# A decode-attention block rebuilt: 32 KB runs for the cache loads, value matmuls on four column groups, and an MLP tail with stationary weights

## The chip, the cores and the metric

The kernel runs on one core of a Trainium2 chip. The metric is device time in microseconds (us); a number for a kernel is the median of its runs. The profile's span is about 1.9 us shorter than that time, because it runs from the first to the last instruction.

## The reference

A batch of 8 single tokens passes an adaptive LayerNorm, attention over a cache of 8,192 positions (32 query heads, 8 key/value heads), an output projection, a second adaptive LayerNorm and an MLP with a squared ReLU.

```python
mod = (silu(c) @ w_mod)                       # six vectors of 512 per token
h = layernorm(x) * (1 + ca) + sa
q = h @ wq                                    # 8 x 32 heads x 128
k, v = repeat(k_cache, 4), repeat(v_cache, 4) # each cache [8, 8, 8192, 128] bf16
o = softmax(q k^T / sqrt(128)) v
x = x + ga * (o @ wo)                         # 4096 -> 512
h = layernorm(x) * (1 + cb) + sb
out = x + gb * (relu(h @ w1 + b1)**2 @ w2 + b2)   # 512 -> 1792 -> 512
```

Each cache holds 134 MB, so the kernel has to move about 284 MB, nearly all of it keys and values that are used once.

## The kernel before

One load is one head of one batch row: 2 MB, in which each of the 128 partitions takes one contiguous run of 16 KB. There are eight ring slots.

```python
src_ap = A_k_cache[kind[1], kind[2]].rearrange("(p t) d -> p t d", p=128)   # values likewise
dst_ap = RING[s][:, :, :]
# ...
ins = sp.dma_start(dst_ap, src_ap)
```

Keys are transposed on TensorE (PE), copied out of PSUM by VectorE (DVE) and ScalarE (ACT), and multiplied with the queries. For the values, each of the 64 tiles of a head is one matmul whose stationary side has four columns (the four query heads that share the values) and whose moving side is 128 columns of V.

```python
for t in range(NT):                                    # 64 tiles per head
    # ... a wait
    qt = (t // 4) % 4
    ins = pe.matmul(Ob[32 * gq:32 * gq + REP, co:co + 128],
                    Pm[:, t, 32 * qt + REP * g:32 * qt + REP * (g + 1)],
                    RING[s][:, t, :], start=(t == 0), stop=(t == NT - 1), tile_position=(0, 32 * gq))
```

The tail keeps the 8 tokens on 8 partitions. The activations are stationary, the weights move, and "fillers" (matmuls whose result nobody reads) keep PE busy between the small steps.

```python
dve.tensor_tensor(t1[:], attn_ps, mod_sb[:, 2 * D:3 * D], ALU.mult)        # 8 x 512
# ... residual and LayerNorm: eight more DVE steps, one ACT step, all on 8 partitions
pe_fill(pe, 48)
# ... four transposes, copy to hbT
for ci, (f0, fl) in enumerate(f_chunks):
    for kt in range(KT_D):
        ins = pe.matmul(hid_flat[:, f0:f0 + fl], hbT[:, kt, :], W1v[:, kt, f0:f0 + fl], ...)
# ... ReLU on ACT, square on DVE, 14 transposes, copy to hidT
for kt in range(KT_F):
    ins = pe.matmul(mlp_ps, hidT[:, kt, :], W2v[:, kt, :], start=False, stop=(kt == KT_F - 1))
```

## Time and profile before

| | before |
|---|---|
| time, median | 703.65 us (703.32 to 704.1, four runs) |
| span of the profiled run | 701.7 us |
| steady rate, 60 to 609.5 us | 426 GB/s |
| instruction packets of the PE queue | 80 |
| last packet of the last value load | 674.1 us |
| from there to the end | 27.6 us |

The landing in the table comes from the trace's packet records (the end of the last packet of that load, counted from the start of the span). It is the number to watch: until it, the kernel waits for data, after it, for the chain of small steps.

These lines are from the page of the kernel before: busy time of the engines, the rows of DMA busy share and rate in 40 slices of the span, and the DMA queues (packets, megabytes, share of the 16 engines' span).

```profile
PE 617.2 (88%) x10113; PEld 528.0 (75%) x10113; DVE 324.6 (46%) x594; ACT 177.7 (25%) x217; POOL 6.2 (1%) x25
DMA  9999999999999999999999999999999999999950
GB/s 354 430 372 429 423 427 425 424 425 428 428 423 425 427 427 424 427 425 426 425 425 426 425 427 423 428 427 424 427 425 425 423 430 424 426 426 427 412 208 1
q1 hardware_dynamic: 26020, 283.68, 96.2%
q8 instruction: 80, 1.31, 0.8%
```

PE is busy 88% of the time, but the DMA engines are busy over 90% in each of the first 38 slices, and from the second slice on the rate stands near 426 GB/s. The third slice (372) holds the load of the output projection's weights, in runs of 1 KB.

The next view cuts the same trace into stretches. Its columns are the stretch, its length, busy time of PE, PEld, DVE, ACT and POOL, the granted PE clock, the DMA share and GB/s.

```profile
60.00:609.50 549.50, 502.13 (x8402) 437.74 (x8400) 260.69 (x466) 146.20 (x180) 0.00 (x0) 0.97 1.01 426
670.00:676.00 6.00, 6.00 (x114) 5.74 (x111) 0.82 (x4) 0.00 (x0) 0.00 (x0) 1.00 0.52 212
676.00:682.00 6.00, 6.00 (x107) 5.61 (x105) 0.72 (x3) 0.00 (x0) 0.00 (x0) 1.00 0.54 191
```

From 670 to 682 us the DMA share is about one half.

How PE handles the values is in one line of the groups (line, engine, operation, output<-inputs, shapes, count; busy time and the mean of one; idle time before):

```profile
L579 PE MATMUL PS<-ring,KTb 128*4 128x128 bf16 x4096 | 221.6, 219 | 8.8 <-DVE rinv L563 5.3
```

There are 4,096 of them with four stationary columns each. Some lines of the timeline of the kernel before show its tail (columns: start, duration, engine, line, operation, output<-inputs, count; in brackets the idle time before it and what ended that).

```profile
682.80 1.89 PE L634 MATMUL PS<-wo_sb,oTn 128*8 128x512 bf16 x8
...
685.89 0.68 DVE L705 BATCH_NORM_STATS2 stats<-x 8x6 f32<-8x512 bf16 x1
...
689.38 3.19 PE L755 MATMUL PS<-ring,hbT 128*8 128x512 bf16 x16
```

The second layer (line 796) is another 14 matmuls of 512 columns in 3.19 us.

### The profile page before, as it was taken

The page shows a single profiled execution, that of the slowest core. Times are in us where ns is not written, and L with a number is a line of the kernel's source. Part 1 is how long each engine was busy: PE and PEld are TensorE (multiplying, and loading weights), DVE is VectorE, ACT ScalarE, POOL GpSimd, SP SyncE. Part 2 cuts the span into 40 slices and gives each one's busy share as a digit, 9 for nine tenths or more (in the row PEclk, how much of TensorE's full clock was granted, in tenths as well). Part 3 has the DMA queues.
Part 4 walks back from the last instruction along what each step waited for, and adds up shares of the span by engine and source line. Part 5 has one row for each costly group of instructions (what it writes and reads, how often), then busy time and mean ns, then how long its engine had stood idle before and what let it go on. Part 6 is the DMA issues. An engine that isn't in the chain of part 4 may idle for free.

```text
span 701.7 us, 21480 instructions
## 1 busy us (share of the span) xinstructions
PE 617.2 (88%) x10113; PEld 528.0 (75%) x10113; DVE 324.6 (46%) x594; ACT 177.7 (25%) x217; POOL 6.2 (1%) x25
## 2 busy tenths in 40 slices
PE   0499799997989799997999899897989989997998
PEld 0187699776977699776987699776977689775984
DVE  1357612774057621766046720676027820676213
ACT  1024510443024410433013320344014420244101
POOL 3000000000000000000000000000000000000000
PEclk9979999999999899999999989999999999999999
DMA  9999999999999999999999999999999999999950
GB/s 354 430 372 429 423 427 425 424 425 428 428 423 425 427 427 424 427 425 426 425 425 426 425 427 423 428 427 424 427 425 425 423 430 424 426 426 427 412 208 1
DMA packets 26109, 285.05 MB, mean 406 GB/s; under 512 B 2187, under 2 KB 8100, under 8 KB 9125
## 3 DMA queue, kind: packets, MB, share of 16 engines
q1 hardware_dynamic: 26020, 283.68, 96.2%
q8 instruction: 80, 1.31, 0.8%
q14 instruction: 9, 0.07, 0.0%
HBM read 283.66 MB, written 0.01 MB: 404 GB/s over the span
## 4 chain that ended last, share of the span: by engine, by line
PE 49%; DMA 38%; DVE 10%; ACT 2%; issue 1%; SPq 0%
DMA ring<-in_A_k_cache_dram 30%; PE PS L439 23%; PE PS L579 14%; PE PS L477 6%; DMA ring<-in_A_v_cache_dram 5%; DVE KTb L413 5%; DMA ring<-in_w_mod_dram 3%; DVE m L501 2%; ACT P_sb L528 2%; PE PS L551 2%; PE PS L292 1%; PE PS L634 1%; PE PS L333 1%; DVE mod_sb L300 0%; PE PS L796 0%
## 5 line engine op out<-in xcount | busy, mean ns | idle before, releaser
L413 DVE COPY KTb<-PS 128x1024 bf16<-128x1024 bf16 x432 | 270.9, 684 | 80.7 <-PE PS L439 79.8
L439 PEld LDWEIGHTS PS<-IDENT,ring 128*128 128x128 bf16 x4096 | 230.7, 98 | 63.1 <-DMA ring<-in_A_k_cache_dram 35.3
L439 PE MATMUL PS<-IDENT,ring 128*128 128x128 bf16 x4096 | 251.2, 220 | 12.9 <-DMA ring<-in_A_k_cache_dram 11.8
L420 ACT ACTIVATE KTb<-PS 128x1024 bf16<-128x1024 bf16 x144 | 147.5, 1024 | 445.2 <-PE PS L439 423.5
L579 PE MATMUL PS<-ring,KTb 128*4 128x128 bf16 x4096 | 221.6, 219 | 8.8 <-DVE rinv L563 5.3
L579 PEld LDWEIGHTS PS<-ring,KTb 128*4 128x4 bf16 x4096 | 218.3, 85 | 10.7 <-DVE rinv L563 6.2
L596 DVE CAST O_sb<-PS 128x256 bf16<-128x256 f32 x7 | 3.0, 425 | 196.3 <-PE PS L579 196.3
L477 PE MATMUL PS<-KTb,QTm 128*32 128x512 bf16 x1024 | 78.8, 384 | 5.3 <-ACT KTb L420 5.3
L551 PE MATMUL PS<-IDENT,P_sb 128*128 128x128 bf16 x512 | 45.1, 271 | 10.2 <-ACT P_sb L528 10.0
L551 PEld LDWEIGHTS PS<-IDENT,P_sb 128*128 128x128 bf16 x512 | 42.8, 126 | 11.8 <-ACT P_sb L528 10.7
L477 PEld LDWEIGHTS PS<-KTb,QTm 128*32 128x32 bf16 x1024 | 15.7, 94 | 21.5 <-DVE KTb L413 9.0
L528 ACT ACTIVATE P_sb<-PS,negm 128x512 bf16<-128x512 f32 x32 | 21.5, 685 | 22.9 <-DVE negm L519 22.9
L501 DVE TENSOR_REDUCE m<-PS 128x1 f32<-128x512 f32 x32 | 19.8, 680 | 0.0
L292 PE MATMUL PS<-ring,csT 128*8 128x512 bf16 x24 | 8.0, 511 | 10.6 <-DMA ring<-in_w_mod_dram 10.6
L609 DVE CAST O_sb<-PS 4x128 bf16<-4x128 f32 x8 | 2.3, 287 | 26.6 <-PE PS L579 26.6
L292 PEld LDWEIGHTS PS<-ring,csT 128*8 128x8 bf16 x24 | 2.5, 107 | 15.7 <-issue 14.6
L511 PEld LDWEIGHTS PS<-Dm,R 128*128 128x128 bf16 x8 | 0.8, 96 | 17.3 <-DVE Dm L505 17.3
L511 PE MATMUL PS<-Dm,R 128*128 128x4 bf16 x8 | 1.4, 179 | 13.3 <-DVE Dm L505 13.3
L535 DVE TENSOR_REDUCE rs<-rs 128x1 f32<-128x4 f32 x8 | 1.3, 157 | 22.8 <-ACT P_sb L528 22.8
L300 DVE CAST mod_sb<-PS 8x3072 bf16<-8x3072 f32 x1 | 3.3, 3345 | 17.5 <-PE PS L292 17.5
L276 PE MATMUL PS<-IDENT,cs 8*128 8x8 bf16 x4 | 0.3, 167 | 10.4 <-DVE cs L250 10.4
L715 ACT ACTIVATE std_<-std_ 8x1 f32<-8x1 f32 x1 | 0.2, 202 | 34.5 <-DVE std_ L709 34.5
(87 smaller groups left out, 98.9 us busy)
## 6 DMA issues: line engine op xcount, KB each, us to landing
ring<-in_A_k_cache_dram SPq DMA_DIRECT2D x64, 2048.0 KB, 30.7
ring<-in_A_v_cache_dram SPq DMA_DIRECT2D x64, 2048.0 KB, 35.0
ring<-in_A_wq_dram SPq DMA_DIRECT2D x2, 2048.0 KB, 9.7
wo_sb<-in_A_wo_dram SPq DMA_DIRECT2D x1, 4096.0 KB, 24.7
ring<-in_B_w_dram SPq DMA_DIRECT2D x2, 1792.0 KB, 24.9
ring<-in_w_mod_dram SPq DMA_DIRECT2D x2, 1536.0 KB, 16.5
x_sb<-in_A_x_dram SPq DMA_DIRECT2D x1, 8.0 KB
c_sb<-in_c_dram SPq DMA_DIRECT2D x1, 8.0 KB
```

The source lines that it names most:

```text
L292: ins = pe.matmul(mod_ps[:, j, :], csT[:, kt, :], wmod_view(kt, j), start=(kt == 0), stop=(kt == KT_D - 1))
L300: s_dve.inc(dve.tensor_copy(mod_sb[:], mod_ps.rearrange("b k n -> b (k n)")))
L333: ins = pe.matmul(QT_ps[:, h, :], wq_view(kt, h), haT[:, kt, :], start=(kt == 0), stop=(kt == KT_D - 1))
L413: v = s_edve.inc(dve.tensor_copy(dst, STG[seq % NSTG]))
L420: v = s_eact.inc(act.activation(dst, STG[seq % NSTG], ACT.Copy))
L439: ins = pe.matmul(STG[seq % NSTG][:, i, :], RING[s][:, t, :], IDENT[:, :], is_transpose=True)
L477: ins = pe.matmul(S_ps[32 * q:32 * (q + 1), k, :], QTm[:, b, g, :], KTb[:, 512 * cch:512 * (cch + 1)], start=(g == 0), stop=(g == HKV - 1) ...
L501: s_dve.inc(dve.tensor_reduce(m4[:, k:k + 1], S_ps[:, k, :], AX.X, ALU.max))
L528: ins = act.activation(P_sb[:, k, :], S_ps[:, k, :], ACT.Exp, bias=negm[:, 0:1], scale=inv_sqrt, accum_out=rs4[:, k:k + 1])
L551: ins = pe.matmul(STG[seq % NSTG][:, i, :], P_sb[:, k, j0:j0 + 128], IDENT[:, :], is_transpose=True)
L579: ins = pe.matmul(Ob[32 * gq:32 * gq + REP, co:co + 128], Pm[:, t, 32 * qt + REP * g:32 * qt + REP * (g + 1)], RING[s][:, t, :], start=(t ...
L634: ins = pe.matmul(attn_ps, oTn[:, h, :], wo_view(h), start=(h == 0), stop=(h == HQ - 1))
```

## The change

The intent is threefold. Two heads are loaded as one 4 MB unit whose runs are 32 KB per partition. Four tiles of values are multiplied by one matmul: 32 stationary columns (four tiles times eight query heads), 512 moving columns, and four such matmuls on the four column groups of the array; a small matmul with a selection matrix then picks the products that belong together. And the tail is transposed: features lie on 128 partitions, the weights are stationary and eight columns move. The program is also written through a helper that places the semaphore waits. The file is nearly all new; this is the core of the difference, with cuts.

```diff
-src_ap = A_k_cache[kind[1], kind[2]].rearrange("(p t) d -> p t d", p=128)
+src = (A_k_cache if kv == "k" else A_v_cache)[b, 2 * p:2 * p + 2]
+src = src.rearrange("g s d -> (g s d)").rearrange("(p f) -> p f", p=128)     # 32 KB a partition, four slots
 # ... value matmuls
-for t in range(NT):
-    ins = pe.matmul(Ob[32 * gq:32 * gq + REP, co:co + 128], Pm[:, t, ...], RING[s][:, t, :], ...)
+for m in range(32):
+    cg = m % 4
+    t = op("tensor", ... e.matmul(Obank[32 * cg:32 * (cg + 1), :], lhs[:, p, 32 * m:32 * m + 32],
+           vt[:, 4 * m:4 * m + 4, :], start=(m < 4), stop=(m >= 28), tile_position=(0, 32 * cg)), ...)
 # ... the very last unit: V stationary, eight columns moving, in chunks of 64, 32, 16, 16 tiles as they land
+pe_fill(70)
+for i, t1 in enumerate(CH):
+    for m in range(t0, t1):
+        t = op("tensor", ... e.matmul(oT_ps, vt[:, m, :], lhs[:, p, 8 * m:8 * m + 8], ...), ...)
+    if i == 0:
+        before_last()        # projection of units 0, 1, 2, and the biases
+    elif i == 1:
+        pe_fill(8)
 # ... MLP
-ins = pe.matmul(hid_flat[:, f0:f0 + fl], hbT[:, kt, :], W1v[:, kt, f0:f0 + fl], ...)
+t = op("tensor", ... e.matmul(hT_ps[hh][:, f % 7, :], wcol(k), hbT[:, k, :], ...), ...)
-ins = pe.matmul(mlp_ps, hidT[:, kt, :], W2v[:, kt, :], ...)
+for cc in range(2):
+    t = op("tensor", ... e.matmul(y_ps[64 * cc:64 * (cc + 1), :], hidT[:, f, :],
+           W2v[:, f // 2, f % 2, 256 * cc:256 * (cc + 1)], ..., tile_position=(0, 64 * cc)), ...)
```

## The prediction

> **What bounds it now.** The DMA. The stage view shows 425 to 426 GB/s in every 78.5 us stretch from 60 to 610 us (one batch row, 33.6 MB, each), with the DMA share at 1.01. The Trainium skill, "DMA: Bandwidth & Descriptors", section "Where 436 GB/s comes from", gives 435 GB/s as the ceiling; the trace agrees. PE is also busy 72 of each 78.5 us, but that is nearly hidden. Two things cost beyond streaming:
>
> 1. Eight of the 16 DMA engines finish late. DMA share is 1.04 at 660 us, about 0.5 from 670 to 682, then zero. The instruction queue moved 80 packets of 16 KB, about 1.07 us each, 86 us in all: if they sit on those eight engines that is 10.7 us each, about the lag. The lagging engines set every landing.
> 2. The tail. The last V load lands near 675.5 us on the slow engines; the kernel ends at 701.7. Those 26 us are PE value matmuls (3.75 us per head, catching up since the softmax at 651), projection, LayerNorm on 8 partitions (DVE 0.4 to 0.7 us per op), MLP with 8 rows stationary (3.2 us per layer), fillers, transposes, output DMA 1.8 us.
>
> **What the change does.**
>
> - Runs of 32 KB. Packet records: 16 KB takes 613 ns, 8 KB 309, 1 KB 49: an estimate from these is 602 ns per 16 KB plus 11 fixed. The skill page, section "Why small descriptors are slow", also names a fixed cost per packet. 512 fewer packets per engine x ~10 ns = about -5 us, all on the critical path.
> - Value matmuls: 128 of 58 ns per pair of heads (7.5 us) become 32 of 512 columns on four column groups, estimated 2 to 3.5 us from the score matmuls (8 in 0.61 us). PE falls from ~72 to ~55 us per batch row: off the critical path, except for the last batch row's backlog.
> - Instructions: my count is about 15.7k instead of 21.5k, so instruction packets shrink by a quarter: about -3 us on the slow engines.
> - Start: two small loads go ahead of the weights, +0.8 us. wo still has 1 KB runs (348 GB/s at 40 to 52 us): unchanged.
> - Tail: last V landing moves to about 668.5 us. From there PE does the rest of the filler, chunk 0, early projection (96 matmuls at 28 ns, as the Q projection's 128 in 3.58 us), last chunks, late projection (about 7 us together), then about twelve small ops on 128 partitions at 0.15 to 0.35 us (3 us), W1 1.6 us, squares 0.4, W2 about 1.2, two adds 0.6, output 1.9: about 16 us. Beside it w1 and w2 land about 9.4 us after V, and need 5 more: nearly as long. Tail saved: about 10 us.
>
> **Sum.** -5 -3 +1 -10 = about -17 us: 686.5 us (-2.4%), range 681 to 692.
>
> **Right if:** steady rate rises to about 429 GB/s; instruction queue near 60 packets; PE busy share falls to 55-65% with granted clock low in value phases; about 16 us between last V landing and end. **Wrong if:** 32 KB packets take twice 613 ns, or HBM dislikes the new pitch (rate below 425); PE in the key phase (10 us per 4 MB against 9.75 us of DMA) gets a cold clock from the idle value phases and falls behind, starving the four-slot ring; the filler of 70 matmuls delays the last unit; or the w2 landing is later than thought.
>
> Chances: faster by over 2%: 0.72; within 2%: 0.25; slower: 0.03.

## More of the kernel before

A load has sixteen landing marks in the trace, one for each DMA engine, and it has landed when the last has come. Of the marks of the last value load, eight came between 658.4 and 663.8 us and eight between 672.9 and 674.6: half of the engines are late by more than 10 us.

The projection ends at 684.7, 10.6 us after the last value landed, because PE still had value matmuls to catch up on. The MLP part takes the last 17.0 us.

## The result

| | before | after |
|---|---|---|
| time, median | 703.65 us | 690.88 us (689.68 to 691.25, four runs) |
| span of the profiled run | 701.7 us | 689.1 us |
| steady rate, 60 to 609.5 us | 426 GB/s | 430 GB/s |
| instruction packets of the PE queue | 80 | 58 |
| last packet of the last value load | 674.1 us | 665.6 us |
| from there to the end | 27.6 us | 23.5 us |

The ratio is 0.9816, with a 95% interval of 0.9802 to 0.983. A ratio here is the mean time of one kernel's fast runs over the mean of the other's fast runs of the same rounds, so it is not quite the ratio of the medians. The kernel is 1.8% faster. All outputs are right. It lies inside the predicted range, but 4.4 us above its centre, and just outside the class that had been favoured (faster by over 2%).

The two landings split the gain: 8.5 us come from data that arrive earlier, 4.1 us from a shorter tail (27.6 less 23.5).

The lines of the page of the kernel after that answer to those above:

```profile
PE 501.7 (73%) x7476; PEld 358.5 (52%) x7476; DVE 300.8 (44%) x557; ACT 235.1 (34%) x281; POOL 17.8 (3%) x67
GB/s 349 442 365 434 429 431 432 427 432 428 425 434 432 432 426 427 429 426 434 435 430 427 430 425 431 433 428 434 425 435 424 428 432 431 433 430 424 421 312 28
q1 hardware_dynamic: 15940, 283.67, 96.7%
q8 instruction: 58, 0.95, 0.6%
```

The same megabytes went in 15,940 packets instead of 26,020, and the rate is some 4 GB/s higher. The slice of the 1 KB runs is as slow as before (365). The stretches of the kernel after, with the columns as above:

```profile
60.00:609.50 549.50, 410.26 (x5837) 285.85 (x5837) 248.84 (x448) 195.89 (x234) 0.00 (x0) 0.82 1.00 430
670.00:676.00 6.00, 3.99 (x110) 3.66 (x107) 0.00 (x0) 0.00 (x0) 0.00 (x0) 0.59 0.36 136
676.00:682.00 6.00, 4.76 (x97) 4.29 (x95) 1.85 (x10) 0.90 (x3) 0.00 (x0) 0.50 0.01 3
```

The value matmuls are now a group of 992 (the last unit, in the thin form, is not among them), which took less than half of the time; the selection matmuls add 22.6 us:

```profile
L442 PE MATMUL PS<-ring,Pm 128*32 128x512 bf16 x992 | 88.3, 519 | 51.7 <-DMA ring<-in_A_v_cache_dram 47.4
```

In the steady part PE works 92 us less, and nothing is gained or lost by it: the DMA share is still 1.00. But the granted clock is down to 0.82, and in the tail, where before it was 1.00, it is 0.5 from 671 us on.

The timeline of the kernel after, from the arrival of the first chunk of the last values to the end:

```profile
661.46 5.37 PE L340 MATMUL PS<-IDENT 128*128 128x128 bf16 x70
666.67 1.75 PE L506 MATMUL PS<-Pm,ring 128*128 128x8 bf16 x64
668.28 2.33 PE L478 MATMUL PS<-oTn,wo_sb 128*128 128x8 bf16 x87
672.62 0.38 PE L478 MATMUL PS<-oTn,wo_sb 128*128 128x8 bf16 x9 [2.01 <-issue]
...
674.62 1.01 PE L340 MATMUL PS<-IDENT 128*128 128x128 bf16 x8
...
676.75 1.02 PE L478 MATMUL PS<-oTn,wo_sb 128*128 128x8 bf16 x32 [0.29 <-DVE oTn L514]
...
681.41 1.68 PE L558 MATMUL PS<-hbT,ring 128*128 128x8 bf16 x56
...
683.02 3.20 PE L566 MATMUL PS<-ring,hidT 128*64 128x256 bf16 x28
```

Three things stand out. The 70 fillers run from 661.5 to 666.8, although the first chunk of values had landed at about 661.2. In the middle of the projection PE stands still for 2.01 us, and the trace gives no instruction as the cause: "issue" means that PE waited for nothing that the profile shows. And the second MLP layer takes 3.20 us, as long as before, although two column groups share its columns.

The tail of 23.5 us is then: the rest of the fillers 1.1, the first chunk and the early projection 3.9, the standstill 2.0, the rest of the projection and the biases 1.1, the other three chunks with eight fillers 2.8, normalisation and late projection 1.3 (together 12.2); the small steps 3.1; a wait behind 16 more fillers 0.4; the first MLP layer 1.7; the second 3.2; the two last DVE steps 0.95; the output 1.9.

### The profile page after: what moved, and what is told of

The parts are those of the page before. It is cut to its first block, busy times and chain, and to the rows that moved or that the text cites. A ratio compares the mean times of both kernels' runs of the same rounds, so it can differ in the third digit from the quotient of the medians.

```text
span 689.1 us, 16075 instructions
## 1 busy us (share of the span) xinstructions
PE 501.7 (73%) x7476; PEld 358.5 (52%) x7476; DVE 300.8 (44%) x557; ACT 235.1 (34%) x281; POOL 17.8 (3%) x67
## 3 DMA queue, kind: packets, MB, share of 16 engines
q1 hardware_dynamic: 15940, 283.67, 96.7%
## 4 chain that ended last, share of the span: by engine, by line
PE 54%; DMA 39%; DVE 3%; ACT 2%; issue 1%; SPq 0%
PE PS L348 35%; DMA ring<-in_A_k_cache_dram 34%; PE PS L363 9%; DMA ring<-in_A_v_cache_dram 4%; PE PS L442 4%; PE PS L405 3%; PE PS L340 1%; ACT KTb L353 1%; ACT P_sb L396 1%; DVE Pm L418 1%; DVE m L368 1%; PE PS L423 1%; PE PS L478 1%; PE PS L506 0%; PE PS L566 0%
## 5 line engine op out<-in xcount | busy, mean ns | idle before, releaser
L353 ACT ACTIVATE KTb<-PS 128x1024 bf16<-128x1024 bf16 x192 | 196.5, 1024 | 384.2 <-PE PS L348 384.2
L348 PE MATMUL PS<-IDENT,ring 128*128 128x128 bf16 x4096 | 267.5, 227 | 49.2 <-DMA ring<-in_A_k_cache_dram 49.2
L355 DVE COPY KTb<-PS 128x1024 bf16<-128x1024 bf16 x320 | 210.1, 688 | 149.5 <-PE PS L348 147.2
L442 PE MATMUL PS<-ring,Pm 128*32 128x512 bf16 x992 | 88.3, 519 | 51.7 <-DMA ring<-in_A_v_cache_dram 47.4
L451 DVE CAST O_sb<-PS 128x512 bf16<-128x512 f32 x31 | 21.4, 692 | 132.5 <-PE PS L442 132.5
L442 PEld LDWEIGHTS PS<-ring,Pm 128*32 128x32 bf16 x992 | 30.8, 121 | 90.2 <-DMA ring<-in_A_v_cache_dram 48.5
L454 PE MATMUL PS<-SEL,O_sb 128*128 128x8 bf16 x124 | 22.6, 182 | 30.4 <-DVE O_sb L451 24.8
L454 PEld LDWEIGHTS PS<-SEL,O_sb 128*128 128x128 bf16 x124 | 12.2, 98 | 59.5 <-DVE O_sb L451 46.1
L405 PE MATMUL PS<-IDENT,P_sb 128*64 128x128 bf16 x512 | 25.7, 276 | 10.3 <-ACT P_sb L396 10.0
L405 PEld LDWEIGHTS PS<-IDENT,P_sb 128*64 128x64 bf16 x512 | 22.1, 147 | 12.9 <-ACT P_sb L396 12.8
L418 DVE COPY Pm<-PS 64x512 bf16<-64x512 bf16 x48 | 20.1, 421 | 16.6 <-PE PS L405 15.6
```

Of the source, the lines that this page charges most:

```text
L348: t = op("tensor", lambda e, j=j, i=i: e.matmul(STG[j][:, i, :], src[:, 32 * k + 8 * j + i, :], IDENT[:, :], is_transpose=True), [loaded[n ...
L353: stg_free[j] = op("scalar", lambda e, j=j, dst=dst: e.activation(dst, STG[j], ACT.Copy), [t])
L355: stg_free[j] = op("vector", lambda e, j=j, dst=dst: e.tensor_copy(dst, STG[j]), [t])
L405: t = op("tensor", lambda e, k=k, i=i, hf=hf, src=src: e.matmul(STG[k][64 * hf:64 * (hf + 1), i, :], src, IDENT[:, :], is_transpose=True, ...
L418: done.append(op("vector", lambda e, dst=dst, frm=frm: e.tensor_copy(dst, frm), [t, k_pm]))
L442: t = op("tensor", lambda e, p=p, m=m, cg=cg, vt=vt, Obank=Obank: e.matmul(Obank[32 * cg:32 * (cg + 1), :], lhs[:, p, 32 * m:32 * m + 32], ...
```

## The experiments

All were edits of the kernel after, unless another parent is named. Ratios are to the kernel before, which ran beside them on the same chip (medians 703.7 to 703.8).

### The 70 fillers

```diff
-                    pe_fill(70)
```

> The changed kernel without the 70 filler matmuls ahead of the last V unit. Theory A (the filler sits on the critical path: chunk 0 of the last unit had landed at about 661.2 us, when the filler began, and PE then ran 5.4 us of filler): 5 us faster or a little more, about 685.5 us, because from there to the end PE never waits for a DMA. Rival B (the filler buys the clock that the tail needs): 0 to 2 us change, because the granted clock falls earlier and the tail stretches. Rival C (the w2 landing bounds the end): no change.

Measured: 684.54 us, ratio 0.9726 (0.9713 to 0.974), 6.3 us less than with the fillers. Lines of this run's timeline:

```profile
661.43 1.85 PE L505 MATMUL PS<-Pm,ring 128*128 128x8 bf16 x64
...
669.48 0.86 PE L505 MATMUL PS<-Pm,ring 128*128 128x8 bf16 x27 [0.89 <-issue]
...
676.88 3.20 PE L565 MATMUL PS<-ring,hidT 128*64 128x256 bf16 x28
```

The first chunk now starts at 661.43, where the fillers had started, and the projection ends 6.2 us after the last landing (665.5) instead of 12.2. Of the 6.3 us, 5.4 are the fillers themselves and about 1.1 a shorter standstill (0.89 for 2.01). The prediction had listed the fillers as a risk but priced them at nearly nothing.

This run also tells what the fillers were for. Its stretches show the clock:

```profile
661.40:664.80 3.40, 3.40 (x128) 3.40 (x129) 0.19 (x1) 0.00 (x0) 0.00 (x0) 0.50 0.85 313
664.80:668.30 3.50, 3.50 (x97) 3.25 (x94) 0.00 (x0) 0.00 (x0) 0.00 (x0) 0.50 0.67 262
```

And these are stretches of the kernel after:

```profile
661.40:664.20 2.80, 2.78 (x28) 2.79 (x29) 0.19 (x1) 0.00 (x0) 0.00 (x0) 0.50 0.75 278
664.20:666.70 2.50, 2.50 (x47) 2.50 (x46) 0.00 (x0) 0.00 (x0) 0.00 (x0) 0.99 0.88 345
666.70:670.60 3.90, 3.90 (x154) 3.84 (x152) 0.00 (x0) 0.00 (x0) 0.00 (x0) 1.00 0.53 210
```

In the kernel after, the clock came to full 2.8 us after the fillers of 128 columns began. In this run PE was busy without a gap for the same time and longer, 6.9 us, with matmuls that nearly all have eight columns (the last 0.8 us are the eight fillers of 128), and the clock stayed at 0.50. The clock record knows only steps of 3.41 us: in both kernels every state but those cut off by the ends lasts a multiple of it. But the thin matmuls gain little from a full clock: 64 of them take 1.75 us after the fillers and 1.85 us without. So the fillers bought speed for work that hardly uses it, and in the kernel after the clock was back at 0.50 at 671.1 us, before the second MLP layer, which could have used it. That the standstill, which began 0.45 us earlier, let it fall is not shown: in two of the runs below (48 extra matmuls, and 8,192 memsets) it fell after a step of 3.41 us in which PE ran thin matmuls without a gap, with no standstill before.

### The 32 KB runs

Each 4 MB load is issued as two of 2 MB with 16 KB per partition.

```diff
-                loaded[n] = dma("sync", s_ring[s], lambda e: e.dma_start(slot(s), src), dep)
+                h = UNIT // 2
+                dma("sync", s_ring[s], lambda e: e.dma_start(RING[:, s, 0:h], src[:, 0:h]), dep)
+                loaded[n] = dma("sync", s_ring[s], lambda e: e.dma_start(RING[:, s, h:UNIT], src[:, h:UNIT]), dep)
```

> The changed kernel with every 4 MB load issued as two of 2 MB with 16 KB per partition, so twice the packets of half the size; same bytes, correct result. Theory A (11 ns of fixed cost per packet, 512 more packets per engine, all on the critical path): 5 us slower, about 696 us, and 427 GB/s in the steady stretches in place of 429.5. Rival B (32 KB runs gave nothing; the gain came from fewer instructions or from PE): same within 1 us.

Measured: 694.53 us, ratio 0.9872 (0.9859 to 0.9886), by the ratios 3.9 us more than the kernel after (3.65 by the medians); the last value landing moved from 665.6 to 670.0 us. Its steady stretch is back at the rate of before:

```profile
60.00:609.50 549.50, 406.96 (x5757) 284.00 (x5757) 245.75 (x443) 193.00 (x231) 0.00 (x0) 0.82 1.01 426
```

The packet records give the reason. A packet of 32 KB takes 1,216 ns in the median, one of 16 KB in the kernel before 613: two small ones cost 10 ns more than one large one. (The run also issues twice as many loads; that is not separated.)

### The instruction count

97 thin matmuls that nobody reads are added to each value unit of the first seven batch rows, so that the program is as long as before.

```diff
+                    for _ in range(0 if lastb else 97):
+                        op("tensor", lambda e: e.matmul(bank(7)[:, 0:8], IDENT[:, :], IDENT[:, 0:8]))
```

> The changed kernel with 97 more matmuls of 8 columns (28 ns) after each of the first 28 V units, where PE idles: 5,432 instructions more, so about 79 instruction packets in place of 58. Theory A (instruction packets sit on eight of the sixteen DMA engines, and those set every landing): 21 packets x 1.07 us / 8 = 2.8 us slower, about 693.7 us. Rival B (instruction packets spread over all engines): 1.4 us slower. Rival C (they cost nothing): 0.

Measured: 694.69 us, ratio 0.9868 (0.9854 to 0.9881), 3.7 us more than the kernel after by the ratios. PE stays hidden in the steady part, and the loads are untouched; what changed is one line of the queues of its page:

```profile
q8 instruction: 80, 1.31, 0.8%
```

22 more instruction packets moved the last landing from 665.6 to 670.1 us, that is 0.2 us for each. I had expected 0.13 (1.07 us per packet, shared by eight engines). A second dose with 48 matmuls instead of 97:

```diff
-                    for _ in range(0 if lastb else 97):
+                    for _ in range(0 if lastb else 48):
```

> The changed kernel with 48 instead of 97 extra matmuls after each of 28 V units: 2,688 instructions, 10 or 11 packets more. If the cost is linear in the packets (22 packets cost 3.8 us): 1.9 us slower than the changed kernel, about 692.8 us. If 97 extra matmuls had put PE itself on the critical path and packets cost little: under 0.7 us.

Measured: 692.28 us (690.28 to 692.91, six runs), ratio 0.9837 (0.9824 to 0.9849); 69 packets; last landing at 668.0. Eleven packets cost 2.4 us of landing, again 0.2 us each, and 1.5 us of time. In the landing the dose is close to linear; the times of this kernel scatter more, and the profiled run was its quickest.

The packet records tell why it is 0.2 and not 0.13. Between 62 and 630 us the kernel after has 53 instruction packets (48 of PE's queue, 1.07 us each) and exactly 53 data packets of 32 KB that took over 1,246 ns, 1,721 on average instead of 1,216. Each of them starts where an instruction packet ends. With the 97 extra matmuls there are 74 and 77. So an instruction packet costs its engine 1.07 us and another 0.5 us in the data packet behind it. Spread over the eight late engines, 1.57 us are 0.2 us. And it is the same eight that move: of the sixteen landing marks of the last values, eight stay at 654 to 659 us with 58, 69 and 80 packets, and the last of the other eight comes at 666.2, 668.5 and 670.5.

A rival said that it is not the packets but PE's work. The thin form of the next section speaks against it: 81 packets, the same late landing, and PE no busier than in the kernel after. To test it directly, instructions were added to an engine that takes no part, POOL:

```diff
+        scr = sb("scr", [128, 64], mybir.dt.uint8)
+        for i in range(5376):
+            t = pool(lambda e, i=i % 256: e.memset(scr[32 * (i % 4):32 * (i % 4) + 1, i // 4:i // 4 + 1], 0),
+                     [t] if i % 256 == 0 else [])
```

> The changed kernel with 5,376 one-byte memsets on the otherwise idle POOL engine, nothing more on PE: about 21 instruction packets more. Theory A (instruction packets as such delay the loads): 3.5 to 4 us slower than the changed kernel, as the run with 5,432 more PE instructions was; about 694.5 us. Rival B (the extra PE work of that run, not the packets, cost the time): no change, 690.9 us. Rival C (only some engines' packets fall on the slow DMA engines): in between, or none.

Measured: 733.17 us, ratio 1.0417. As designed this missed: POOL got through one one-byte memset in about 130 ns (5,376 of them fill the span), so it was itself the last to end and set the time. The landing can still be read. The packets of the page's queue:

```profile
q8 instruction: 58, 0.95, 0.5%
q14 instruction: 50, 0.41, 0.1%
```

PE did nothing more and its 58 packets stayed, but the other instruction queue rose from 8 packets to 50, and the last value landing moved from 665.6 to 683.5 us. So something that an idle engine does can delay the loads. Its instructions are the likely cause: here too each of the 39 packets of that queue between 62 and 630 us is followed by a long data packet. The size, 18 us for 42 packets of 8 KB, does not fit 0.2 us each, but of the sixteen landing marks of the last values fifteen came by 667.9 us and one at 684.0: a single engine was late, so nothing was shared. The memsets' own writes are a second possible cause that this run does not exclude, and 105 more long data packets follow no instruction packet and stay unexplained. It was repeated with 8,192 memsets (the range 5376 changed to 8192):

> The same with 8,192 memsets on POOL, 32 packets more. Theory A (linear, 0.18 us per packet): 5.8 us slower than the changed kernel, 696.6 us. Rival B: no change. If POOL takes over 80 ns per memset it ends near the end of the kernel, and the run says nothing.

Measured: 1102.76 us. Here POOL ended about 400 us after everything else (the output was written near 703 us). The memsets came at the same pace as before, so the landing, at 682.8 us, had been exposed to no higher dose than in the run before; the run says nothing about the dose.

### The form of the value matmuls

The kernel after, with its value matmuls made thin everywhere: V stationary, eight columns moving, one tile each.

```diff
-                    for m in range(32):
-                        cg = m % 4
-                        t = op("tensor", ... e.matmul(Obank[32 * cg:32 * (cg + 1), :], lhs[:, p, 32 * m:32 * m + 32],
-                            vt[:, 4 * m:4 * m + 4, :], ..., tile_position=(0, 32 * cg)), ...)
+                    for m in range(128):
+                        t = op("tensor", ... e.matmul(oT_ps, vt[:, m, :], lhs[:, p, 8 * m:8 * m + 8], ...), ...)
```

> The changed kernel with the value matmuls of all units in the form that its last unit has: 128 one-tile matmuls with V stationary (8 columns moving) per pair of heads, no column groups, no copy and no selection matmuls. About 5,700 instructions more. Theory A (PE is off the critical path in the value phases, only instruction packets count): 3 us slower, as the run with more instructions. Rival B (the four column groups are what made the kernel faster): 5 us slower or more. Rival C: faster, if the copy and selection matmuls were on the path.

Measured: 695.48 us, ratio 0.9885 (0.9872 to 0.9899). It has 81 instruction packets, and its last landing, 670.1 us, is that of the lengthened program with the four column groups. Its steady stretch, PE busy 406 us:

```profile
60.00:609.50 549.50, 406.45 (x8337) 342.27 (x8338) 226.59 (x415) 193.00 (x231) 0.00 (x0) 0.76 1.00 429
```

PE is no busier than in the kernel after (410 us). So the four column groups were worth about as much as their shorter program, and nothing as faster arithmetic: PE had not been the limit.

### The order of the tail

No fillers at all, and the projection of units 0 and 1 with the first layer's bias moved to before unit 2, where PE waits for data anyway.

```diff
+                if lastb and p == 2:
+                    before_third()      # project(rows_of(0) + rows_of(1), ...) and the first bias
 # ...
-                        project(early, True, False, ...)       # and the first bias
+                        project(rows_of(2), False, False, [norm_last])
-                    pe_fill(70)
-                            pe_fill(8)
-        pe_fill(16, 3)
```

> The changed kernel with the PE work around the last V unit reordered: no filler matmuls at all, the projection rows of units 0 and 1 and the first bias moved into the PE idle time before unit 2, only the rows of unit 2 between chunk 0 and chunk 1. Theory A (what follows the last landing at about 666.2 us sets the end): the late projection ends about 3 us earlier than in the run without the 70 fillers (670.4 to about 667 us for the last value matmul) until the w2 landing (about 675.5 us) binds: end about 680 us of span, 681.5 us measured. Rival B (w2 landing already bound the run without the filler): 684 to 685 us.

Measured: 682.87 us, ratio 0.9704 (0.9691 to 0.9718), 8.0 us less than the kernel after. From the timeline of this run:

```profile
667.34 0.65 PE L511 MATMUL PS<-Pm,ring 128*128 128x8 bf16 x19 [1.79 <-issue]
668.02 0.19 DVE L517 TENSOR_TENSOR oTn<-PS,rinv 128x8 bf16<-128x8 f32 x1 [6.45 <-PE PS L511]
...
674.27 3.31 PE L568 MATMUL PS<-ring,hidT 128*64 128x256 bf16 x28
```

The standstill stayed, but moved: here it comes after 45 of the 64 value matmuls of the last three chunks. In three kernels it stands beside an instruction packet of the packet records. Kernel after: packet from 670.1 to 671.2, standstill from 670.6 to 672.6. Without the 70 fillers: 666.9 to 668.0, and 668.6 to 669.5. Here: 664.8 to 665.9, and 665.55 to 667.34. Each time PE goes on 1.4 to 1.5 us after the packet's end. The Trainium skill, "Runtime: NRT & Kernel Launch", section "Instruction fetch mechanics", says that an engine's instruction memory is refilled in blocks of 16 KiB, 256 instructions. The trace agrees: 7,476 matmuls with a weight load each are 14,952 instructions, 58.4 blocks, and the queue moved 58 packets of 16 KB.

If the standstill is a late refill, it must move when the program is shifted by half a block. 64 thin matmuls (128 instructions with their weight loads) were put one batch row earlier, into the kernel of the new order:

```diff
+                    for _ in range(64 if (b, p) == (B - 2, 1) else 0):
+                        op("tensor", lambda e: e.matmul(bank(7)[:, 0:8], IDENT[:, :], IDENT[:, 0:8]))
```

> The reordered kernel with 64 more matmuls of 8 columns (128 instructions, half an instruction packet) in an idle stretch of PE one batch row before the end. In the reordered kernel PE stood still for 1.8 us after 46 of the last 64 value matmuls, with no wait that the profile shows, while an instruction packet came in. Theory A (PE had run out of instructions at a packet boundary): the same standstill comes 64 matmuls earlier, after about 16 of the 32 projection matmuls of unit 2, or vanishes because PE waited long enough before. Rival B (it waits for the chunk's data or for something in that place of the program): it stays where it is.

Measured: 682.55 us in one single run of unknown state; its span, 680.5 us, is that of its parent (680.4). From its timeline:

```profile
663.62 1.85 PE L513 MATMUL PS<-Pm,ring 128*128 128x8 bf16 x64
...
666.60 1.87 PE L513 MATMUL PS<-Pm,ring 128*128 128x8 bf16 x64
```

The 64 matmuls of the last chunks run without a gap, and the packet comes at 660.8 to 661.9, earlier than it is needed. That speaks against the rival, that something at this place in the program makes PE wait, though it is one look; and in the kernel after the standstill was in the projection, which waits for no load. But nothing was gained: PE reached the last unit 2.4 us later. It was 1.4 us late already in the softmax (642.0 for 640.6), and the first value unit took 3.33 us at a clock of 0.50 instead of 1.91 at 1.00.

### The second MLP layer

The second layer on four column groups of 128 columns instead of two of 256, on top of the new order (the tensors that it uses are laid out likewise).

```diff
-            for cc in range(2):
+            for cc in range(4):
                 t = op("tensor", ... e.matmul(
-                    y_ps[64 * cc:64 * (cc + 1), :], hidT[:, f, :], W2v[:, f // 2, f % 2, 256 * cc:256 * (cc + 1)], ...
+                    y_ps[32 * cc:32 * (cc + 1), :], hidT[:, f, :], W2v[:, f // 2, f % 2, 128 * cc:128 * (cc + 1)], ...
```

> The run before with the second MLP layer on four column groups of 128 columns instead of two of 256 (56 matmuls instead of 28, half the column time at the low clock), so smaller adds and four output DMAs. Theory A (at the granted clock of 0.5 the columns are what costs: 28 matmuls in 3.2 us): this layer takes 1.7 us and the adds 0.3 us less, output issue 0.4 us more: about 1.4 us faster than the run before, unless w2 lands after it is needed, then 0.5 us. Rival B (the layer waits for instructions or weight loads): no gain.

Measured: 681.52 us, ratio 0.9686 (0.9673 to 0.9699), 1.4 us less than its parent. Its layer in the timeline:

```profile
674.17 1.04 PE L568 MATMUL PS<-ring,hidT 128*32 128x128 bf16 x32
...
675.82 0.83 PE L568 MATMUL PS<-ring,hidT 128*32 128x128 bf16 x24 [0.61 <-DMA ring<-in_B_w_dram]
```

The matmuls fell from 3.3 to 1.9 us, and 0.6 us of that went into a new wait: the last landing mark of the second half of w2 is at 675.8. The tail is now at the edge where DMA limits it again.

The other way to a faster layer would be a full clock. Five fillers of 512 columns were put into the gaps of the LayerNorm:

```diff
+        def wide_fill(n):
+            for _ in range(n):
+                op("tensor", lambda e: e.matmul(bank(3)[:, :], IDENT[:, :], wo_sb[:, 0, :]))
+        wide_fill(1)      # and again 1 and 3 further on
```

> The reordered kernel with five filler matmuls of 512 columns between the small operations of the LayerNorm. Theory A (the low granted clock at the end comes from matmuls of 8 columns, which keep the array busy for a small part of the time): the records show the granted clock back at 1.0 before or in the second MLP layer, which then takes 1.6 us instead of 3.2 us: up to 1.5 us faster than the reordered kernel. Rival B (3 us of fill come too late for the clock): no gain, or 0.3 us slower from the fill itself.

Measured: 683.24 us, ratio 0.971 (0.9697 to 0.9723), no gain over its parent. From its stretches and its timeline:

```profile
669.00:675.00 6.00, 5.65 (x102) 3.53 (x101) 2.29 (x12) 0.90 (x3) 0.00 (x0) 0.50 0.45 172
```

```profile
675.17 3.20 PE L574 MATMUL PS<-ring,hidT 128*64 128x256 bf16 x28
```

PE was busy 5.65 of 6 us and the clock stayed at 0.50. The rule by which the clock comes back is not settled by these runs. What they show is that busy time alone is not it. In the parent the second layer's own matmuls (674.27 to 677.58) brought the clock back, at 677.69, when they had just ended.

### The best version

The new order, the four column groups, and the two small first loads issued from another engine, so that they no longer stand ahead of the weights in the queue of the large loads.

```diff
-        d_c = dma("sync", s_c, lambda e: e.dma_start(c_sb, c))
-        d_x = dma("sync", s_x, lambda e: e.dma_start(x_sb, A_x.rearrange("b s d -> (b s) d")))
+        d_c = dma("scalar", s_c, lambda e: e.dma_start(c_sb, c))
+        d_x = dma("scalar", s_x, lambda e: e.dma_start(x_sb, A_x.rearrange("b s d -> (b s) d")))
```

> The kernel with four column groups in the second MLP layer, and c and x loaded from the other issuing engine, so that the first weight load is issued about 0.8 us earlier. Theory A (the DMA stream now sets both ends: first issue and w2 landing): 0.6 us faster, about 680.9 us. Rival B (the end is set by PE): no change.

Measured: 681.12 us (680.9 to 682.15), ratio 0.968 (0.9667 to 0.9694): 3.2% less than the kernel before and 9.8 us less than the kernel after. The last landing is at 664.5 us, 0.7 earlier than in its parent. The time that this gained, 0.4 us, is within the spread of the runs. This version, too, still has the standstill (1.96 us, from 665.3).

## Why the prediction was right or wrong

**Right: the limit and its rate.** DMA bounds both kernels. 429 GB/s was predicted and 430 came. The fixed cost per packet of the Trainium skill, "DMA: Bandwidth & Descriptors", section "Why small descriptors are slow", is there in the trace: 1,216 ns for 32 KB against twice 613. The predicted 5 us for the larger runs were 3.9.

**Right in kind, too small in size: the instructions.** Packets fell to 58 (60 predicted). The 3 us were 3.7 us of time and 4.5 us of landing, 0.2 us for each packet where 0.13 had been assumed. The term that was too small is the packet's price, taken as its own 1.07 us; the 0.5 us that it adds to the data packet behind it were missing.

**Right in kind: the landing.** It was to move by 7 us (675.5 to 668.5) and moved by 8.5 (674.1 to 665.6). The two experiments that undo a part, 4.5 us each, add up to 9.0; the slower start (1 us predicted) would account for the 0.5 us between, and the best version, which undoes it, lands 0.7 us earlier than its parent.

**Right: the value matmuls are off the critical path.** The thin form, everywhere, moved the landing only by its instructions.

**Wrong: the tail.** The step that failed is "Tail saved: about 10 us"; 4.1 us were saved. Its terms were predicted at 15.7 us in sum and measured 23.5:

- "the rest of the filler, chunk 0, early projection [...], last chunks, late projection (about 7 us together)" took 12.2 us. This is the main miss. PE reached the 70 fillers only when the data behind them had landed, so nearly all of their 5.4 us lay on the critical path; and a late instruction block held PE for 2.0 us. The kernel before has no such standstill in its tail; its value matmuls follow each other every 58 ns (64 in 3.75 us) where those of the new tail do so every 28, which may be why (not tested). Without the fillers the same part took 6.2 us, so the price of the work itself had been about right.
- "W2 about 1.2" took 3.2 us, because the clock was at 0.50 and not at 1.00. The starts of the matmuls show it: before, one of 512 columns every 214 ns at a clock of 1.00; after, two of 256 columns together every 213 ns at 0.50; on four groups, four of 128 every 105 ns at 0.50. The halved columns and the halved clock cancelled exactly (3.19 before). At the full clock it would have been 1.6 us, an estimate from the pace before, so 1.2 was too low as well.
- The small steps (3 predicted, 3.1 measured), the first layer (1.6 and 1.7) and the output (1.9) were right. The intent of the transposed tail was met: from the end of the projection to the end of the kernel it is 17.0 us before and 11.3 after. What it gained there was partly lost between landing and the end of the projection: 10.6 us before, 12.2 after.

**Wrong, without effect: PE's share.** 55 to 65% were predicted, 73% came. The prediction's own 55 us of 78.5 per batch row would be 70%; 58.6 were measured. The selection matmuls, 22.6 us in all, had not been priced, and at the lower clock (0.97 to 0.82 in the steady part) the key transposes took 268 us instead of 251. The feared starvation of the ring did not follow: the DMA share stayed 1.00.

In sum: about 3.9 us from the runs, 3.7 from the instructions and 5 from the rest, mostly the tail, make 12.8. The class was decided by 70 matmuls that compute nothing: without them the kernel is at 0.9726.

**Left open:** why an instruction packet makes the data packet behind it 0.5 us longer; how much of the POOL run's delay is instructions and how much its writes; and by what rule the clock rises.

## What to carry to other kernels

In a kernel that DMA bounds, the length of the program is data too: each 256 instructions on PE cost 0.2 us of landing here, and where matmuls last 28 ns the next block of instructions can come too late. Before leaving fillers in, look at when PE reaches them and when the data behind them has landed, and whether the work that follows is wide enough to use the clock that they buy. When a tail is rebuilt, price it at the clock and in the order in which PE will really arrive there, not at the clock of the old tail.

## What the Trainium skill lacked or had wrong

- "Runtime: NRT & Kernel Launch", section "Instruction fetch mechanics", calls the cost of crossing a 16 KiB boundary "one DMA tail-bump, mostly hidden". Its block size agrees (58 packets for 14,952 instructions). Its cost does not: 22 blocks more moved the last landing by 4.5 us and the time by 3.7, and PE stood still for 0.9 to 2.4 us where thin matmuls ran. No page gives the price of such a packet for the data's engines: 1.07 us here, and 0.5 us more in the data packet behind it.
- "TensorE: Matmul & The Clock Gate", Part 1, says that about 3.4 us of sustained matmul activity bring the full clock, and that this is a budget of time, not of matmuls. 128-column fillers did it 2.8 us after they began, which is no contradiction: the record's step of 3.41 us had begun at 660.8 us, and PE was busy in all of it. But matmuls of eight columns did not in 6.9 us without a gap (0.50 throughout), nor did 5.65 busy us of 6 with five 512-column fillers among thin ones. The page lacks what counts as activity.
- "DMA: Bandwidth & Descriptors", section "Why small descriptors are slow", finds joining consecutive descriptors in one packet worth it only at 256 bytes or less. It does not say what longer runs are worth far above that, which is another thing: here one run of 32 KB in place of two of 16 KB saved 10 ns in 1,226, and with it 3.9 us of 694.5.
